# Second chunk's weights: the row term of the log sums as a bias of ScalarE, head by head

## The chip, the cores and the metric

The kernel runs on one core of a Trainium2 chip. The metric is the device time of one execution in microseconds; the times are medians over several runs, lower is better. The engines are called TensorE (PE in the profile, PEld its weight loads), VectorE (DVE), ScalarE (ACT), GpSimd (POOL) and SyncE (SP), which issues the DMAs.

## What is computed

An mLSTM over 4 batches, 8 heads, 768 steps and head size 40, and behind it a feed-forward layer with ELU (320 to 2048 to 320, over 3072 tokens). Cut to what matters:

```
for t in range(S):
    m_new  = max(f_gate[t] + m, i_gate[t])
    f_stab = exp(f_gate[t] + m - m_new);  i_stab = exp(i_gate[t] - m_new);  m = m_new
    C = f_stab * C + i_stab * outer(v[t], k[t])
    n = f_stab * n + i_stab * k[t]
    y[t] = sigmoid(o_gate[t]) * (C @ q[t]) / max(|n . q[t]|, 1)
h = x @ w_in                      # x: y with the heads side by side
out = elu(h) @ w_out
```

## The kernel before

The 768 steps are cut into six chunks of 128, and each chunk and batch is a tile, n = 4 * chunk + batch, so tiles 4 to 7 belong to the second chunk (c = 1). Inside a chunk the recurrence is written as attention: a tile multiplies keys by queries (`products`, L627: eight heads, in two PSUM buffers by parity of the head), multiplies that element by element by weights w[s, t] (L692), and multiplies the weighted products with the values (`outputs`, L712 for the state carried in, L720 inside the chunk, L730 for the state carried out). Then come the denominators (L764 to L769), the gate (L777, L781), a transpose by TensorE (`turn`, L795) and its split into a rounded and a rest part (xh, xl; L803 to L812, with L805 on TensorE in the first two tiles).

The weights of one head are w[s, t] = exp(a[t] + b[s]) for s <= t and 0 elsewhere, where a[t] is the running sum of the log decays and b[s] = i[s] - a[s]. For the first two chunks (LOGS = 2) they are made so. `gate_chunk` holds all 32 pairs of batch and head in the partitions and puts a into lc[:, 0] (L506) and b into lc[:, 1] (L510), 128 columns each. Because the matmuls that follow are in bf16, both are split into three bf16 parts, stacked in lcs (three casts, with two subtractions between them, L524; all of 256 columns). `spread`, once for each half of a tile (four heads), builds a + b + mask in a PSUM buffer of 512 columns: one matmul for the mask (L658), one for b, which picks the row of each head with the selection matrix sel (L662), and four of 128 columns for a (L668). One exponential on ScalarE (L683) then writes the half's weights to SBUF. Its last columns are copied to wl, and wl scales the values for the state (L696).

In the later chunks the weights come from a scan on VectorE (L675) and the source factors are transposed by TensorE (L542), copied to iT (steps in the partitions, batch and head in the columns) and multiplied into the values.

PSUM has three rings: ps_a with three buffers, h with two (the log sums of a half, the first layer's result h, and the differences of L379 and L380, which belong to the conversion of the weights) and acc with three (the opening matmuls L418, which only keep TensorE busy, and the second layer, L875).

The order of the instructions on each engine is no compiler's: every operation is handed to a planner with a cost for each engine that can do it (`op({"PE": 0.8}, ...)`), the keys that it reads and those that it writes. The planner runs a small simulation: at each moment it starts, of the operations that are ready, the one with the best rank (rank of the tile or conversion, then the longest rest of its chain), on the engine where it would start first. The order in which they start is the order of each engine's queue, and on the chip each engine works through its queue in order. Ranks of the first tiles and conversions stand in FIRST = "t0t1t2t4c5c0c4c3": tile 4 is begun before tile 3. Two of the conversions of w_in and w_out into a rounded and a rest part (L337 to L371 on ScalarE, VectorE and GpSimd, L379 and L380 with a difference on TensorE) are needed by each group of steps of the first layer (L848) and the second layer (L875).

Of the kernel before, what the change touches and what calls it, by code (L numbers as in the profile page):

```python
# [14 lines left out]
AF = mybir.ActivationFunctionType  # L15
# [5 lines left out]
P = 128  # L21
# [17 lines left out]
class Plan:  # L39
# [23 lines left out]
    def op(self, engines, fn, r=(), w=(), nbytes=0):  # L63
        port = "port" in engines
        engines = {e: x for e, x in engines.items() if e != "port"}
        o = Op(engines, fn, {k[:2] for k in (*r, *w)}, nbytes, port)
        o.rank = self.rank
        for k in r:
            if k in self.writer:
                o.before.add(self.writer[k])  # L70
            self.readers.setdefault(k, []).append(o)
        for k in w:
            if k in self.writer:
                o.before.add(self.writer[k])
            o.before.update(self.readers.pop(k, ()))
            self.writer[k] = o
        o.before.discard(o)
        for b in o.before:
            b.after.add(o)
        self.ops.append(o)  # L80
        return o
# [110 lines left out]
def tile_mlstm_then_elu_ffn(  # L192
# [9 lines left out]
    nc = tc.nc  # L202
    PSUM = bass.MemoryType.PSUM
    B, NC, R3, _, HH, L = qk.shape
# [4 lines left out]
    BH = B * H  # L209
# [7 lines left out]
    W2N = 2  # L217

    LOGS = 2
    LOG_MIN = -104.0  # L220
    MASKED = -(2.0**100)

# [19 lines left out]
    op = plan.op  # L242
    eng = {"PE": nc.tensor, "DVE": nc.vector, "ACT": nc.scalar, "POOL": nc.gpsimd, "SP": nc.sync}

    def copy(e, o, i):
        nc.scalar.copy(o, i) if e == "ACT" else eng[e].tensor_copy(o, i)
# [8 lines left out]
    def act(n):  # L255
        return {"ACT": 0.17 + 0.00088 * n}
# [213 lines left out]
    def gate_chunk(c):  # L470
        def f():
            return T("gates", c, BH, 2, L, part="fi")[:, 0]

        def i():
            return T("gates", c, BH, 2, L, part="fi")[:, 1]

        def m():
            return T("gates", c, BH, L + 1, part="m")

        KF, KI, KM, FI = ("gates", c, "f"), ("gates", c, "i"), ("gates", c, "m"), ("first", 0)  # L480

        op({"ACT": 0.2, "DVE": 0.13}, lambda e: copy(e, m()[:, 0:1], m0), (("m0", 0),), (KM,))
        op({"port": 1, "DVE": 0.48},
           lambda e: nc.vector.tensor_tensor_scan(
               m()[:, 1:], f(), i(), m0, op0=ALU.add, op1=ALU.max),
           (KF, KI, ("m0", 0)), (KM,))
        op({"ACT": 0.2, "DVE": 0.13}, lambda e: copy(e, m0, m()[:, L : L + 1]), (KM,), (("m0", 0),))

        def log_decay(e):
            nc.vector.tensor_add(f(), f(), m()[:, 0:L])  # L490
            nc.vector.tensor_sub(f(), f(), m()[:, 1:])
            if c < LOGS:
                nc.vector.tensor_scalar_max(f(), f(), LOG_MIN)

        op({"port": 1, "DVE": 0.6 if c >= LOGS else 0.84}, log_decay, (KM,), (KF,))
        op({"port": 1, "POOL": 0.4, "DVE": 0.27}, lambda e: eng[e].tensor_sub(i(), i(), m()[:, 1:]), (KM,), (KI,))
        if c < LOGS:

            def lc():
                return T("gates", c, BH, 2, L, part="lc")  # L500

            KLC = ("gates", c, "lc")

            def sums_of_logs(e):
                nc.vector.memset(lc()[:, 0, 0:1], 0.0)
                nc.vector.tensor_tensor_scan(  # L506
                    lc()[:, 0, 1:], f()[:, 1:], first[:, 1:], 0.0, op0=ALU.add, op1=ALU.min)

            op({"port": 1, "DVE": 0.53}, sums_of_logs, (KF, FI), (KLC,))
            op({"port": 1, "DVE": 0.27}, lambda e: nc.vector.tensor_sub(lc()[:, 1], i(), lc()[:, 0]), (KI,), (KLC,))  # L510
            if c > 0:
                op({"ACT": 0.35},
                   lambda e: nc.scalar.activation(i(), lc()[:, 0], AF.Exp, bias=f()[:, 0:1]), (KLC, KF), (KI,))
                op({"SP": 0.4}, lambda e: nc.sync.dma_start(b_d[c], i()), (KI,), (("b_d", c),),
                   nbytes=BH * L * 4)

            n = 2 * L
            for j in range(3):
                part = lcs[j * BH : (j + 1) * BH, c]
                op({"port": 1, "ACT": 0.2 + 0.00092 * n, "DVE": 0.29},  # L520
                   lambda e, part=part: copy(e, part, lc()), (KLC,), (("lcs", c, j),))
                if j < 2:
                    op({"port": 1, "DVE": 0.41},
                       lambda e, part=part: nc.vector.tensor_sub(lc(), lc(), part), (("lcs", c, j),), (KLC,))  # L524
            return
        op({"ACT": 0.3}, lambda e: nc.scalar.activation(f(), f(), AF.Exp), (), (KF,))
        op({"ACT": 0.3}, lambda e: nc.scalar.activation(i(), i(), AF.Exp), (), (KI,))

        def starts(e):

            nc.vector.tensor_copy(first[:, 0:1], f()[:, 0:1])
            nc.vector.memset(f()[:, 0:1], 0.0)

        op({"port": 1, "DVE": 0.2}, starts, (KF,), (FI, KF))
        op({"SP": 0.4}, lambda e: nc.sync.dma_start(f_d[c], f()), (KF,), (("f_d", c),),
           nbytes=BH * L * 4)

        def turned():
            return T("ps_a", ("iT", c), P, BH)

        KT = ("ps_a", ("iT", c))
        op({"PE": 0.24}, lambda e: nc.tensor.transpose(turned(), i(), ident[:BH, :BH]),  # L542
           (KI, ("ident", 0)), (KT,))
        op({"DVE": 0.19, "ACT": 0.25}, lambda e: copy(e, iT[:, c, :], turned()),
           (KT,), (("iT", c),))

        op({"port": 1, "DVE": 0.42},
           lambda e: nc.vector.tensor_tensor_scan(
               i(), f(), first, 0.0, op0=ALU.mult, op1=ALU.add),
           (KF, FI), (KI,))  # L550
        op({"SP": 0.4}, lambda e: nc.sync.dma_start(b_d[c], i()), (KI,), (("b_d", c),),
           nbytes=BH * L * 4)
# [32 lines left out]
    def attention(n):  # L585
# [18 lines left out]
        def w(half=None):  # L604
            a = T("w", n, P, H * L).rearrange("p (h t) -> p h t", t=L)
            return a if half is None else a[:, half * HH : (half + 1) * HH, :]
# [43 lines left out]
        for half in range(2):  # L650
            KW, KP = ("w", n, half), ("h", ("w", n, half))

            def logs(half=half):
                return T("h", ("w", n, half), P, HH, L)

            def spread(e, half=half, logs=logs):
                mine = [b * H + h for h in heads[half * HH : (half + 1) * HH]]
                nc.tensor.matmul(  # L658
                    logs(), ident_b, mask.unsqueeze(1).to_broadcast([P, HH, L]),
                    start=True, stop=False, skip_group_check=True,  # L660
                )
                nc.tensor.matmul(  # L662
                    logs(), lcs[:, c, 1],
                    sel[:, mine[0] : mine[-1] + 1 : 2].unsqueeze(2).to_broadcast([3 * BH, HH, L]),
                    start=False, stop=False, skip_group_check=True,
                )
                for j, r in enumerate(mine):
                    nc.tensor.matmul(  # L668
                        logs()[:, j, :], sel[:, r : r + 1].to_broadcast([3 * BH, P]), lcs[:, c, 0],
                        start=False, stop=(j == HH - 1), skip_group_check=True,  # L670
                    )

            def decays(e, half=half):
                a = w(half).rearrange("p h t -> p (h t)")
                nc.vector.tensor_tensor_scan(  # L675
                    a, a, ident4.rearrange("p h t -> p (h t)"), 0.0, op0=ALU.mult, op1=ALU.add
                )

            if c < LOGS:
                op({"PE": 0.8}, spread,  # L680
                   (("sel", 0), *(("lcs", c, j) for j in range(3)), ("mask", 0), ("ident_b", 0), ("w", n, "room")), (KP,))
                op(act(HH * L),
                   lambda e, half=half, logs=logs: nc.scalar.activation(w(half), logs(), AF.Exp), (KP,), (KW,))  # L683
            else:
                op({"port": 1, "DVE": 1.23}, decays, (("ident4", 0),), (KW,))

            if c < NC - 1:
                op({"POOL": 0.3, "DVE": 0.17, "ACT": 0.2},
                   lambda e, half=half: copy(e, wl()[:, half::2], w(half)[:, :, L - 1]),
                   (KW,), (("wl", n, half),))  # L690
            op(two_ps(HH * L),
               lambda e, half=half: nc.vector.tensor_mul(w(half), ps(half, P, HH, L), w(half)),  # L692
               (("ps_a", (n, half)),), (KW,))
# [319 lines left out]
```

## Time and profile before

| | us |
|---|---|
| median of 3 runs | 472.73 |
| lowest and highest of them | 469.61, 473.63 |
| the profiled execution's own time | 471.69 |
| its span in the profile | 469.8 |

The profile shows one execution. Its span goes from the first to the last instruction; the execution's own time has some 1.9 us more around it. Start times are in microseconds from the start of the span. "Idle before" is the time that an engine stood still in front of an instruction, with the instruction that ended the wait behind the arrow; "issue" means that nothing in the profile shows what it waited for. An arrow between two names (out<-in) says what is written from what.

### The profile page before, as it was taken

To read this page: it belongs to the slowest core of one execution; us is meant where nothing else is said; L and a number is where in the kernel's file an instruction comes from. 1 tells how busy PE (TensorE), PEld (TensorE's weight loads), DVE (VectorE), ACT (ScalarE), POOL (GpSimd) and SP (SyncE) were. 2 spreads that over 40 slices of the span, in tenths; PEclk is the share of its full clock that TensorE was granted. 3 is DMA by queue.
4 is the path that set the end of the run, shared out by engine and by line. 5 is a ranking of instruction groups with operands and counts; after the bars stand their busy time and mean duration, and the time that the engine had idled before them with its cause. 6 is when DMAs were issued, how large, how long until landed. Compare 5 with 4: busy or idle time off the path is not lost.

```text
span 469.8 us, 13709 instructions
## 1 busy us (share of the span) xinstructions
PE 454.2 (97%) x5700; PEld 426.3 (91%) x5700; DVE 340.0 (72%) x705; ACT 284.0 (60%) x701; POOL 94.7 (20%) x122
## 2 busy tenths in 40 slices
PE   6978999999999999999999999999999999999996
PEld 3757798999999999998899999999999999999995
DVE  6887888987878898688888885487448754464443
ACT  7776886688776547464654455545546455545563
POOL 2323353422311052234102220030010200000000
PEclk9888999999999999999999999999999999999999
DMA  8878644522407364248243532044113401000100
GB/s 241 312 209 269 190 153 143 179 100 95 140 2 220 97 189 128 74 155 228 64 142 108 161 119 83 1 129 127 42 31 102 144 1 43 0 3 1 43 0 31
DMA packets 39391, 52.85 MB, mean 112 GB/s; under 512 B 2880, under 2 KB 31264, under 8 KB 39328
## 3 DMA queue, kind: packets, MB, share of 16 engines
q1 hardware_dynamic: 39328, 51.97, 36.3%
q8 instruction: 45, 0.74, 0.7%
q14 instruction: 18, 0.15, 0.1%
HBM read 46.56 MB, written 5.39 MB: 111 GB/s over the span
## 4 chain that ended last, share of the span: by engine, by line
PE 88%; DVE 4%; ACT 3%; DMA 2%; issue 1%; SPq 0%; POOL 0%; POOLq 0%; ACTq 0%
PE h L848 37%; PE acc L875 35%; PE ps_a L627 5%; PE ps_a L720 3%; PE ps_a L712 3%; PE ps_a L795 2%; DMA wide<-in_w_in 2%; PE ps_a L730 1%; DVE gl L866 1%; ACT e L856 1%; ACT e L859 0%; DVE w L371 0%; PE h L379 0%; DVE w L675 0%; ACT narrow L337 0%
## 5 line engine op out<-in xcount | busy, mean ns | idle before, releaser
L848 PE MATMUL h<-xh,w 128*128 128x384 f32 (+1 forms) x720 | 178.8, 323 | 0.8 <-DVE e L861 0.8
L875 PE MATMUL acc<-w,gh 128*128 128x320 f32 x768 | 172.9, 311 | 1.4 <-ACT gh L864 0.9
L875 PEld LDWEIGHTS acc<-w,gh 128*128 128x128 f32 x768 | 128.2, 188 | 3.6 <-ACT gh L864 1.2
L848 PEld LDWEIGHTS h<-xh,w 128*128 128x128 f32 x720 | 125.4, 189 | 3.0 <-DVE e L861 1.3
L875 PE MATMUL acc<-w,gl 128*128 128x320 f32 x384 | 118.7, 309 | 1.2 <-DVE gl L866 1.2
L861 DVE SCALAR_TENSOR_TENSOR e<-e,h 128x384 f32<-128x384 f32 (+1 forms) x144 | 72.7, 506 | 62.4 <-ACT e L859 60.2
L856 ACT ACTIVATE e<-h 128x384 f32<-128x384 f32 (+1 forms) x144 | 65.4, 454 | 83.2 <-PE h L848 75.8
L848 PE MATMUL h<-xl,w 128*128 128x384 f32 (+1 forms) x432 | 112.0, 318 | 0.0
L866 DVE TENSOR_TENSOR gl<-e,gh 128x384 fp32r<-128x384 f32 (+1 forms) x130 | 70.8, 550 | 34.2 <-ACT gh L864 33.1
L864 ACT CAST gh<-e 128x384 fp32r<-128x384 f32 (+1 forms) x144 | 67.8, 474 | 33.3 <-DVE e L861 32.9
L848 PEld LDWEIGHTS h<-xl,w 128*128 128x128 f32 x432 | 77.0, 190 | 0.0
L875 PEld LDWEIGHTS acc<-w,gl 128*128 128x128 f32 x384 | 72.0, 188 | 1.7 <-DVE gl L866 1.7
L859 ACT ACTIVATE e<-e 128x384 f32<-128x384 f32 (+1 forms) x144 | 70.5, 490 | 3.5
L675 DVE TENSOR_TENSOR_SCAN w<-w,ident 128x512 f32<-128x512 f32 x32 | 40.5, 1275 | 0.4 <-DMA w<-f_d 0.3
L361 POOL TENSOR_TENSOR narrow<-narrow,wide 128x512 int32<-128x512 int32 (+1 forms) x18 | 27.4, 1520 | 60.5 <-DVE narrow L356 37.5
L747 POOL TENSOR_TENSOR C<-C,dec 40x164 f32<-40x164 f32 x26 | 14.5, 556 | 99.7 <-PE ps_a L712 96.9
L692 DVE TENSOR_TENSOR w<-ps_a,w 128x512 f32<-128x512 f32 x48 | 31.8, 682 | 2.8 <-PE ps_a L627 2.5
L627 PE MATMUL ps_a<-qk 40*128 40x128 f32 x384 | 29.0, 290 | 0.0
L627 PEld LDWEIGHTS ps_a<-qk 40*128 40x128 f32 x384 | 24.2, 192 | 4.5 <-issue 2.5
L866 POOL TENSOR_TENSOR gl<-e,gh 128x256 fp32r<-128x256 f32 (+1 forms) x14 | 12.4, 886 | 64.9 <-ACT gh L864 61.3
L720 PE MATMUL ps_a<-vko,w 128*32 128x41 f32 x1536 | 20.7, 207 | 0.3 <-DVE vko L637 0.3
L720 PEld LDWEIGHTS ps_a<-vko,w 128*32 128x32 f32 x1536 | 18.7, 114 | 1.7 <-issue 0.9
(113 smaller groups left out, 414.0 us busy)
## 6 DMA issues: line engine op xcount, KB each, us to landing
vko<-in_vko SPq DMA_DIRECT2D x24, 484.0 KB
qk<-in_qk SPq DMA_DIRECT2D x24, 448.0 KB
w<-f_d SPq DMA_DIRECT2D x32, 256.0 KB
wide<-in_w_out SPq DMA_DIRECT2D x8, 640.0 KB
wide<-in_w_in SPq DMA_DIRECT2D x8, 512.0 KB
out<-os SPq DMA_DIRECT2D x24, 160.0 KB
bb<-b_d SPq DMA_DIRECT2D x40, 80.0 KB
sum<-os SPq DMA_DIRECT2D x8, 160.0 KB
```

Source lines behind the costliest of these rows:

```text
L361: lambda e: nc.gpsimd.tensor_add(narrow(), narrow(), words()[0]),
L627: nc.tensor.matmul(ps(two, P, HH, L)[:, j, :], kt[rows, j, :], qt[rows, j, :], start=True, stop=True,)
L675: nc.vector.tensor_tensor_scan(a, a, ident4.rearrange("p h t -> p (h t)"), 0.0, op0=ALU.mult, op1=ALU.add)
L692: lambda e, half=half: nc.vector.tensor_mul(w(half), ps(half, P, HH, L), w(half)),
L720: nc.tensor.matmul(y[r, h, :], w()[:, i, r], va()[:, h, :], start=not opened, stop=(i == H - 1), skip_group_check=True,)
L848: nc.tensor.matmul(h(), a[g][:, fs], m, start=(i == 0), stop=(i == len(prods) - 1))
L856: op(act(N), lambda e, h=h, ff=ff: nc.scalar.activation(ff("e"), h(), AF.Relu, scale=-1.0), (KHP,), (KE,))
L859: lambda e, ff=ff: nc.scalar.activation(ff("e"), ff("e"), AF.Exp, scale=-1.0), (), (KE,))
L861: lambda e, h=h, ff=ff: nc.vector.scalar_tensor_tensor(out=ff("e"), in0=ff("e"), scalar=-1.0, in1=h(), op0=ALU.add, op1=ALU.max),
L864: op(act(N), lambda e, ff=ff: nc.scalar.copy(ff("gh", F32R), ff("e")), (KE,), (KG,))
L866: lambda e, ff=ff: eng[e].tensor_sub(ff("gl", F32R), ff("e"), ff("gh", F32R).bitcast(F32)),
L875: nc.tensor.matmul(acc(a), x[:, sl], bw[g][:, j, :], start=(f == f0 and i == 0), stop=(f == f1 - 1 and i == 2),)
```

## The change

For chunks from APART = 1 on that are weighted by log sums, which is the second chunk alone:

- only a, 128 columns of lc, is split into bf16 parts; the three casts and two subtractions run on half the columns, with their costs in the plan left as they were;
- b, in f32 as L510 leaves it, is transposed by TensorE into a buffer of the ring acc (cost in the plan 0.01) and copied by ScalarE to iT (0.01), as soon as L510 is done;
- `spread` leaves out the matmul of L662, its cost in the plan is unchanged;
- the exponential of a half is four instructions, one for each head, of 128 columns, with the head's column of iT as bias; the cost in the plan is that of the one instruction.

```
     LOGS = 2
+    APART = 1
...
+            apart = c >= APART
...
+            KLS = ("ls", c)
+            op({"port": 1, "DVE": 0.27}, lambda e: nc.vector.tensor_sub(lc()[:, 1], i(), lc()[:, 0]),
+               (KI,), (KLC, KLS))
...
-            n = 2 * L
+            n = L if apart else 2 * L
             for j in range(3):
-                part = lcs[j * BH : (j + 1) * BH, c]
-                op({"port": 1, "ACT": 0.2 + 0.00092 * n, "DVE": 0.29},
-                   lambda e, part=part: copy(e, part, lc()), (KLC,), (("lcs", c, j),))
+                part = lcs[j * BH : (j + 1) * BH, c, 0:1] if apart else lcs[j * BH : (j + 1) * BH, c]
+                op({"port": 1, "ACT": 0.2 + 0.00184 * L, "DVE": 0.29},
+                   lambda e, part=part: copy(e, part, lc()[:, 0 : n // L]), (KLC,), (("lcs", c, j),))
                 if j < 2:
                     op({"port": 1, "DVE": 0.41},
-                       lambda e, part=part: nc.vector.tensor_sub(lc(), lc(), part), (("lcs", c, j),), (KLC,))
+                       lambda e, part=part: nc.vector.tensor_sub(
+                           lc()[:, 0 : n // L], lc()[:, 0 : n // L], part), (("lcs", c, j),), (KLC,))
+            if apart:
+
+                def sources():
+                    return T("acc", "sources", P, BH)
+
+                KT = ("sources", c)
+                op({"PE": 0.01}, lambda e: nc.tensor.transpose(sources(), lc()[:, 1], ident[:BH, :BH]),
+                   (KLS, ("ident", 0)), (KT,))
+                op({"ACT": 0.01}, lambda e: copy(e, iT[:, c, :], sources()), (KT,), (("iT", c),))
...
-                nc.tensor.matmul(
-                    logs(), lcs[:, c, 1],
...
+                if c < APART:
+                    nc.tensor.matmul(
+                        logs(), lcs[:, c, 1],
...
-               op(act(HH * L),
-                  lambda e, half=half, logs=logs: nc.scalar.activation(w(half), logs(), AF.Exp), (KP,), (KW,))
+                def weigh(e, half=half, logs=logs):
+                    if c < APART:
+                        nc.scalar.activation(w(half), logs(), AF.Exp)
+                        return
+                    for j, r in enumerate(heads[half * HH : (half + 1) * HH]):
+                        nc.scalar.activation(w(half)[:, j], logs()[:, j], AF.Exp, bias=ib[:, r])
+
+                op(act(HH * L), weigh, (KP,) + ((("iT", c),) if c >= APART else ()), (KW,))
```

## Rows read from the trace of the kernel before

**Rows 1.** The page's first part: busy time of each engine, share of the span, number of instructions.

```profile
PE 454.2 (97%) x5700; PEld 426.3 (91%) x5700; DVE 340.0 (72%) x705; ACT 284.0 (60%) x701; POOL 94.7 (20%) x122
```

**Rows 2.** Two stretches of the span (from:to, length), with each engine's busy time and number of instructions, then TensorE's granted clock, the DMA engines' share and GB/s.

```profile
0.00:71.30 71.30, 61.52 (x1006) 46.25 (x1006) 56.37 (x143) 53.96 (x136) 23.72 (x34) 0.93 0.76 230
71.30:200.00 128.70, 128.64 (x1469) 125.65 (x1470) 107.85 (x218) 86.05 (x209) 36.85 (x38) 1.00 0.39 123
```

**Rows 3.** Pieces of the chain of work that ended last, from 27 to 43 us: start, how long the piece holds the chain, engine, tile, line and number of instructions.

```profile
27.44 1.25 PE ps_a L720 x64
28.69 0.59 PE ps_a L730 x32
...
35.26 0.22 PE h L662
...
38.08 0.74 PE ps_a L720 x64
38.82 0.29 PE ps_a L730 x32
...
40.95 1.88 issue
```

**Rows 4.** Groups of instructions by line, engine, operation and shape: number, busy time in us, mean ns of one, idle time before them. The second row is from the view of the one line L662: ns of the shortest, median and longest, first and last start.

```profile
L683 ACT ACTIVATE w<-h 128x512 f32<-128x512 f32 x16 | 9.2, 585 | 0.3 <-PE h L668 0.2
L662 PE MATMUL h<-sel,lcs x16: 379/381/534, 7.0 to 58.2; 96*128 96x512 bf16 x16
L513 ACT ACTIVATE gatesfi<-gateslc,gatesfi 32x128 f32<-32x128 f32 x1 | 0.4, 385 | 0.0
L526 ACT ACTIVATE gatesfi<-gatesfi 32x128 f32<-32x128 f32 x4 | 1.2, 298 | 0.1
L246 ACT COPY iT<-ps_a 128x32 f32<-128x32 f32 x3 | 0.5, 175 | 0.0
L542 PE MATMUL ps_a<-ident,gatesfi 32*128 32x32 f32 x4 | 1.0, 244 | 0.0
L524 DVE TENSOR_TENSOR gateslc<-gateslc,lcs 32x256 f32<-32x256 f32 x4 | 1.6, 412 | 0.1
L510 DVE TENSOR_TENSOR gateslc<-gatesfi,gateslc 32x128 f32<-32x128 f32 x2 | 0.6, 280 | 0.1
L246 DVE CAST lcs<-gateslc 32x256 bf16<-32x256 f32 x5 | 1.4, 272 | 0.1
```

**Rows 5.** Instructions in order of time, from 30 to 39 us: start, length (of the whole run where there are several), engine, line, operation, number, and idle time before it.

```profile
30.51 0.60 ACT L683 ACTIVATE w<-h 128x512 f32<-128x512 f32 x1
31.51 0.60 ACT L683 ACTIVATE w<-h 128x512 f32<-128x512 f32 x1
32.59 0.48 ACT L246 CAST xh<-ps_a 128x384 fp32r<-128x384 f32 x1 [0.26 <-PE ps_a L795]
34.88 0.38 PE L658 MATMUL h<-mask,ident_b 128*128 128x512 bf16 x1 [0.56 <-DVE w L246]
35.56 1.06 ACT L683 ACTIVATE w<-h 128x512 f32<-128x512 f32 x2
38.11 0.59 ACT L246 CAST w<-h 128x512 fp32r<-128x512 f32 x1 [1.26 <-PE h L380]
```

**Rows 6.** The same view from 22 to 30 us. The last row is the first spread of the second chunk.

```profile
22.39 1.57 PE L627 MATMUL ps_a<-qk 40*128 40x128 f32 x16
23.37 0.28 DVE L510 TENSOR_TENSOR gateslc<-gatesfi,gateslc 32x128 f32<-32x128 f32 x1
25.00 0.52 PE L795 MATMUL ps_a<-ident,xf 128*128 128x128 f32 x3 [1.04 <-DVE xf L781]
26.00 1.29 DVE L692 TENSOR_TENSOR w<-ps_a,w 128x512 f32<-128x512 f32 x2
26.24 0.46 ACT L246 CAST xh<-ps_a 128x384 fp32r<-128x384 f32 x1
26.75 0.69 PE L805 MATMUL ps_a<-xh,minus 128*128 128x384 f32 x1 [1.24 <-ACT xh L246]
29.17 0.61 PE L658 MATMUL h<-mask,ident_b 128*128 128x512 bf16 x1
```

**Rows 7.** The same view of ScalarE and TensorE alone, from 54 to 72 us.

```profile
54.85 0.62 ACT L367 CAST w<-narrow 128x512 fp32r<-128x512 f32 x1 [0.47 <-POOL narrow L361]
56.09 0.58 ACT L683 ACTIVATE w<-h 128x512 f32<-128x512 f32 x1
56.81 1.10 PE L379 MATMUL h<-narrow,ident 128*128 128x512 f32 x2
58.17 0.59 ACT L246 CAST w<-h 128x512 fp32r<-128x512 f32 x1 [0.79 <-PE h L380]
63.98 0.39 ACT L856 ACTIVATE e<-h 128x256 f32<-128x256 f32 x1 [0.88 <-PE h L848]
71.36 0.56 PE L875 MATMUL acc<-w,gh 128*128 128x320 f32 x2 [0.45 <-DVE w L371]
```

**Rows 8.** Three stretches, columns as in rows 2.

```profile
24.00:26.00 2.00, 0.52 (x3) 0.34 (x3) 1.87 (x8) 1.87 (x7) 0.00 (x0) 1.00 0.20 47
26.00:28.00 2.00, 1.25 (x39) 0.92 (x43) 1.96 (x4) 1.63 (x5) 0.00 (x0) 0.62 0.75 211
28.00:30.00 2.00, 2.00 (x78) 1.40 (x68) 1.18 (x3) 0.85 (x3) 1.28 (x1) 0.53 1.00 294
```

More of the change, by code (lines that the diff above doesn't have):

```diff
@@ L509, in gate_chunk @@
             op({"port": 1, "DVE": 0.53}, sums_of_logs, (KF, FI), (KLC,))
-            op({"port": 1, "DVE": 0.27}, lambda e: nc.vector.tensor_sub(lc()[:, 1], i(), lc()[:, 0]), (KI,), (KLC,))
+            KLS = ("ls", c)
+            op({"port": 1, "DVE": 0.27}, lambda e: nc.vector.tensor_sub(lc()[:, 1], i(), lc()[:, 0]),
+               (KI,), (KLC, KLS))
             if c > 0:
@@ L661, in spread @@
                 )
-                nc.tensor.matmul(
-                    logs(), lcs[:, c, 1],
-                    sel[:, mine[0] : mine[-1] + 1 : 2].unsqueeze(2).to_broadcast([3 * BH, HH, L]),
-                    start=False, stop=False, skip_group_check=True,
-                )
+                if c < APART:
+                    nc.tensor.matmul(
+                        logs(), lcs[:, c, 1],
+                        sel[:, mine[0] : mine[-1] + 1 : 2].unsqueeze(2).to_broadcast([3 * BH, HH, L]),
+                        start=False, stop=False, skip_group_check=True,
+                    )
                 for j, r in enumerate(mine):
```

## Prediction

> **What bounds the kernel now.** I read the page's busy times first: TensorE is busy for 97% of the span, ScalarE for 60% [rows 1]. An average over stages hides what matters here, so next I cut the span by stage. From 71.3 us on TensorE has no gap to speak of (128.64 busy of 128.70), and its clock is granted in full; before 71.3 us it is busy for 61.52 of 71.30 and has a granted clock of 0.93 [rows 2]. So the end comes at a fixed distance behind the moment at which TensorE gets into its stride, and only what shifts that moment moves the end. All work of the second chunk's weights lies before it: the eight spreads (tiles 4 to 7, two halves each) lie between 29.2 and 58.4 us [rows 4, 6]. In that stage the chain of waits changes between VectorE, ScalarE and TensorE, and so an edit pays only where it lies on this chain.
>
> **Prices.** What goes: eight matmuls of 512 columns. One occupies TensorE for 0.22 us before the next matmul starts [rows 3] (its own 381 ns overlap the neighbours [rows 4]): 8 x 0.22 = 1.76 us. What comes on TensorE: one transpose of 32x128, as the later chunks' transposes at 0.244 us [rows 4]. Net -1.5 us.
>
> VectorE: the two subtractions shrink from 256 to 128 columns, 0.412 to the 0.280 that a subtraction of 32x128 takes, 2 x -0.13. Of the three casts two are on VectorE at 0.272; halved they save between nothing and half of that, 0.14; I take -0.1 each; in all -0.45 us [rows 4]. ScalarE gets one copy of iT, 0.175 [rows 4], and its one cast of lcs gets about 0.1 shorter.
>
> ScalarE's exponentials are the large term. One half is now one instruction of 585 ns. It becomes four of 128 columns with a bias for each partition. The trace has no such form. The nearest rows are an exponential of 32x128 without a bias, 298 ns, and one of the same size with a bias from a column, 385 ns [rows 4]. Two exponentials in a row end 1.06 us after the first starts [rows 5], so neighbours overlap by 2 x 0.585 - 1.06 = 0.11. With the row that has a bias: 4 x 0.385 - 3 x 0.11 = 1.21, so +0.62 a half and +5.0 over eight. Lower end, the bias hidden behind the instruction before: 4 x 0.298 - 3 x 0.11 = 0.86, +0.28 a half and +2.2. Upper end, no overlap at all: 4 x 0.385 = 1.54, +0.96 a half and +7.7. Below nothing it can't go, as the same elements are read with three more starts. I take +0.62, the row that shares the form. By the Trainium skill (ScalarE: Activation LUTs, "What ACT_TABLE_LOAD costs"), each column operand adds some 93 ns and back-to-back instructions overlap by the same; an estimate from that page is 4 x 387 - 3 x 93 = 1.27 against 612 for the wide one, +0.66 a half and +5.3 in all. The rule speaks against the edit, and the trace shows 87 ns for the bias and 585 for the wide one.
>
> So by busy time the edit loses: 5 us of ScalarE for 1.5 of TensorE. What counts is where they fall.
>
> **From 22 to 30 us.** The transpose waits for the subtraction of L510, which ends at 23.65; TensorE reaches the products of the third tile (L627) at 22.39 [rows 6]. By the costs in the code the planner puts the transpose ahead of these products, because in its plan they start after that subtraction. Then TensorE, which works in order, stands still from 22.45 to 23.65, and the 16 products behind the transpose start at 23.9 and end at 25.5 in place of 23.96. Who waits for that? The transposes of L795 (25.00) move to 25.5, but their reader, the ScalarE cast of xh, starts only at 26.24, behind two conversion steps on its own engine. The multiplication L692 needs the products, and starts at 26.00 because VectorE is busy with the log sums until then; these get 0.45 shorter, so it can start at 25.55, just behind the products. So the stall is covered by the idle time of 1.04 before L795 and of 1.24 before L805 [rows 6], which the trace has anyway; without this cover it would cost 1.3. L692 ends 0.45 earlier, L805 stays where it is, and the outputs (L720, on the chain at 27.44) start 0.4 earlier. Bounds: 0 (the iT copy delays xh) to -0.45. I take -0.4. If the transpose stands behind the products, the result is the same. Its PSUM buffer comes from a ring that only the opening matmuls have used by then and the second layer uses later, so nobody waits for it.
>
> **From 30 to 43 us.** Tile 4's first exponential (30.51) is on the chain [rows 5]: -0.4 + 0.62 = +0.2 for the copy behind it and for the unbroken VectorE work up to the spread at 34.88. The second half (31.51) adds some 0.1 through the copy of its last column, since ScalarE has only 0.26 idle ahead of xh (32.59). The spread then starts 0.3 late, and with its row matmul gone it ends 0.1 late. Tile 5's two halves (35.56) add 1.24 to ScalarE, and the 1.26 that it waits at 38.11 for TensorE cover them [rows 5]. The stop of 1.88 us inside L712, with no releaser, I leave as it is [rows 3]: it starts in the middle of a block whose operands are there. So +0.1 at 43 us.
>
> **From 53 to 71 us.** Tile 6's first half costs 0.62 against 0.47 of idle time at 54.85: 0.15 is left [rows 7]. Its second half (56.09) is the place that counts: TensorE's L379 (56.81) takes the PSUM buffer that this exponential reads, of two in that ring, so it starts 0.7 late, and whatever the shorter spreads just before it saved is waited away there. Tile 7's first half is covered by the 0.79 that ScalarE waits at 58.17 for that same L379, now later too. Its second spread gives back 0.22, so +0.5 goes into the first layer; its second exponential (61.09) is covered by 0.88 of idle time at 63.98 [rows 7]. At 71.36 the second layer [rows 7] starts behind a conversion that hangs on the same ScalarE and VectorE work and is late by as much. From there TensorE hands it on to the end.
>
> Sum: -0.4 + 0.5 + 0.5 = +0.6 us. The profiled execution took 471.69 us (span 469.8 and 1.9 around it), so 472.3; the median of the runs shown lies 1.04 above it, which gives **473.3**. With the low price of the exponentials the sum is -0.3 (472.4 in medians), with the high one near +2 (474.7).
>
> **Rivals.**
> *The clock is kept: faster.* After TensorE was busy for only 0.52 of 2 us, its granted clock was 0.62 and then 0.53, near the lower of its two levels (1.2 of 2.4 GHz), from 26 to 30 us [rows 8]. The outputs took 1.25 and 0.59 there and 0.74 and 0.29 at 38 us in full clock [rows 3]. If the products that move into the gap keep the clock up, the chain gets 0.8 shorter: with the low price -0.3 - 0.8 = -1.1, 471.6. Against it: the gap isn't gone but lies earlier, and a fall at another place would cost as much. The Trainium skill (TensorE: Matmul & The Clock Gate, "Part 1: The HAM clock gate") says that the throttled state is the default and activity lifts it; by that less matmul work could lose clock, and here the fall behind the gap agrees.
> *ScalarE becomes the bound: slower.* It is one place, ScalarE's queue from 30 to 62 us. Where its idle time (0.26, 1.26, 0.47, 0.79 and 0.88 [rows 5, 7]) doesn't lie behind the halves that it has to cover, all +5.0 is on the path, less 0.4 and two row matmuls: +4.2, 476.9. It decides from about 0.8 a half on. For it speaks that exponentials hold buffers that TensorE wants; against it, that it still waits for other engines at these five places.
> *The order isn't what it was.* The new operations cost 0.01 in the plan, but a shift can swap neighbours. One swap is worth about one of the waits of this stage, 1.0 to 1.9 [rows 3, 6], either way: 471.4 to 475.2.
>
> **How the numbers follow.** Forecast 0.55, clock kept 0.2, ScalarE the bound 0.1, another order 0.12; 0.03 for the rest. The runs shown spread from 469.61 to 473.63, which is as wide as the cases, so the range goes beyond them a little: 470.2 to 477.0. A change below 1% (4.7 us) can't be told from none in a measurement of this kernel; beyond it on the slow side lie ScalarE's upper price and part of its rival (0.08), on the fast side a lucky order with a kept clock (0.04).
>
> **What would show it.** Exponentials of 128 columns near 0.38 us, 32 of them, and a half taking 1.2; TensorE idle before a transpose that ends near 23.9; L720 near 27.0; the spread of 34.88 near 35.2; L379 of 56.81 near 57.5 behind ScalarE; no gap of TensorE after 72. It is wrong if the second layer's unbroken run starts over 3 us away from 71.4, if a half takes under 0.8, or if TensorE's order before 70 us differs.

## The result and the profile after

| kernel | median, us | lowest to highest | runs |
|---|---|---|---|
| before | 472.74 | 468.49 to 474.58 | 22 |
| after | 476.04 | 472.83 to 478.87 | 22 |

The ratio is 1.0079, 95% interval 1.0054 to 1.0105. The change costs 3.3 us by the medians, 3.7 by the ratio. That is inside the predicted range and below 1%, but the sum said +0.6. The prediction held that a change below 1% can't be told from none in this kernel; with 22 runs on each side this one can.

The profiled execution of after took 472.83 us (span 470.7, granted clock 0.992). It is the shortest of its 22, so its span must not be set against that of before; what can be read from it are prices, order and gaps.

The page of after: first the busy times, to be read against [rows 1].

```profile
PE 452.3 (96%) x5693; PEld 424.6 (90%) x5693; DVE 339.2 (72%) x705; ACT 288.4 (61%) x726; POOL 94.8 (20%) x122
...
q8 instruction: 44, 0.72, 0.7%
```

TensorE has 7 matmuls and 7 weight loads fewer, ScalarE 25 instructions and 4.4 us more, as the edit says. The last row looks like nothing here (transfers, MB, share of 16 DMA engines' span); it is one of two queues of the kind "instruction", and the experiments will tie it to TensorE's program. Before has the row below. The 45th transfer of after starts behind the end of its span, at 471.83.

```profile
q8 instruction: 45, 0.74, 0.7%
```

Groups of after by line and shape, against [rows 4] (number, busy us, mean ns of one, idle time before):

```profile
L703 ACT ACTIVATE w<-h,iT 128x128 f32<-128x128 f32 x32 | 9.0, 370 | 0.0
L700 ACT ACTIVATE w<-h 128x512 f32<-128x512 f32 x8 | 4.6, 583 | 0.2
L528 DVE TENSOR_TENSOR gateslc<-gateslc,lcs 32x128 f32<-32x128 f32 x2 | 0.6, 276 | 0.0
L247 DVE CAST lcs<-gateslc 32x128 bf16<-32x128 f32 x2 | 0.4, 188 | 0.0
L536 PE MATMUL acc<-ident,gateslc 32*128 32x32 f32 x1 | 0.2, 243 | 0.0
```

The 32 new exponentials keep ScalarE busy for 9.0 us, where eight wide ones at 0.585 took 4.7.

Timeline of after from 22 to 39 us, rows against [rows 5] and [rows 6] (L641 is the old L627, L672 the old L658, L714 the old L692, L734 the old L712, L742 the old L720, L752 the old L730, L817 and L827 the old L795 and L805; L380 and L381 the old L379 and L380):

```profile
22.39 1.57 PE L641 MATMUL ps_a<-qk 40*128 40x128 f32 x16
...
24.98 0.52 PE L817 MATMUL ps_a<-ident,xf 128*128 128x128 f32 x3 [1.01 <-DVE xf L803]
...
25.42 0.24 PE L536 MATMUL acc<-ident,gateslc 32*128 32x32 f32 x1
25.63 1.29 DVE L714 TENSOR_TENSOR w<-ps_a,w 128x512 f32<-128x512 f32 x2
...
26.23 0.46 ACT L247 CAST xh<-ps_a 128x384 fp32r<-128x384 f32 x1
...
26.74 0.69 PE L827 MATMUL ps_a<-xh,minus 128*128 128x384 f32 x1 [1.07 <-ACT xh L247]
...
27.35 1.32 PE L742 MATMUL ps_a<-vko,w 128*32 128x41 f32 x64
```

The transpose (L536) follows the products and L817; nothing waits for it. L714 is 0.37 earlier than L692 was, and still the outputs start where they did, at 27.35 for 27.37; before has this row:

```profile
27.37 1.32 PE L720 MATMUL ps_a<-vko,w 128*32 128x41 f32 x64
```

```profile
30.49 1.14 ACT L703 ACTIVATE w<-h,iT 128x128 f32<-128x128 f32 x4
...
32.01 1.17 ACT L703 ACTIVATE w<-h,iT 128x128 f32<-128x128 f32 x4
```
```profile
35.65 0.38 PE L672 MATMUL h<-mask,ident_b 128*128 128x512 bf16 x1 [1.05 <-DVE w L247]
```
```profile
36.33 2.14 ACT L703 ACTIVATE w<-h,iT 128x128 f32<-128x128 f32 x8
...
38.91 0.59 ACT L247 CAST w<-h 128x512 fp32r<-128x512 f32 x1 [0.21 <-PE h L381]
```

A half takes 1.14 in place of 0.60. The spread of 34.88 starts at 35.65, and the idle time of 1.26 before the cast has shrunk to 0.21. The same view of ScalarE and then of TensorE from 55 us on, against [rows 7]:

```profile
55.67 1.12 ACT L703 ACTIVATE w<-h,iT 128x128 f32<-128x128 f32 x4
```
```profile
56.89 1.10 PE L380 MATMUL h<-narrow,ident 128*128 128x512 f32 x2 [1.10 <-issue]
```

TensorE stands still for 1.10 us until tile 6's exponentials release the buffer at 56.79. The view puts the wait down to "issue"; the end of the run above it, 55.67 + 1.12, is what the matmul follows.

Two stretches of after, the second to be set beside its row of before below:

```profile
71.30:200.00 128.70, 128.62 (x1468) 125.53 (x1469) 107.65 (x218) 85.85 (x209) 36.84 (x38) 1.00 0.40 123
160.00:215.00 55.00, 54.47 (x876) 51.72 (x875) 44.46 (x94) 29.41 (x91) 18.34 (x24) 1.00 0.49 147
```
```profile
160.00:215.00 55.00, 55.00 (x883) 52.45 (x882) 44.87 (x95) 30.10 (x92) 19.28 (x25) 1.00 0.50 151
```

Before has no gap of TensorE from 160 to 215 us; after has 0.53 us. Nearly all of it is one stop, in the middle of a block of equal matmuls, and the view shows nothing that TensorE waited for (timeline of TensorE, after and then before):

```profile
207.13 0.44 PE L752 MATMUL ps_a<-vko 128*8 128x41 f32 x25
208.09 0.27 PE L752 MATMUL ps_a<-vko 128*8 128x41 f32 x6 [0.51 <-issue]
```
```profile
206.94 0.49 PE L730 MATMUL ps_a<-vko 128*8 128x41 f32 x31
```

Matching the two traces instruction by instruction, after lies within 0.01 us of before all the way from 71 to 173 us, drops back by 0.2 at 174 and by 0.7 at 207, and keeps the difference to the end. That is new: a loss behind 72 us, where the change edits nothing and the prediction wanted no gap of TensorE.

That the second layer starts at 71.37 against 71.36, although 30 to 58 us lost time, has another cause. From 44 to 46 us the granted clock was 1.00 in this execution of after and 0.50 in that of before:

```profile
44.00:46.00 2.00, 2.00 (x54) 1.93 (x41) 1.28 (x5) 1.47 (x5) 0.82 (x1) 1.00 0.85 284
```
```profile
44.00:46.00 2.00, 2.00 (x30) 1.90 (x20) 1.28 (x5) 1.04 (x3) 0.05 (x1) 0.50 0.66 225
```

In 2 us of unbroken work it did 54 matmuls for 30. All runs taken together don't share this: the median of the granted clocks is 0.984 to 0.985 for after and 0.986 to 0.988 for before.

### The profile page after: what moved, and what is told of

It is laid out like the page before. It is cut to its first block, busy times and chain, and to the rows that moved or that the text cites. A ratio compares the mean times of both kernels' runs of the same rounds, so it can differ in the third digit from the quotient of the medians.

```text
span 470.7 us, 13721 instructions
## 1 busy us (share of the span) xinstructions
PE 452.3 (96%) x5693; PEld 424.6 (90%) x5693; DVE 339.2 (72%) x705; ACT 288.4 (61%) x726; POOL 94.8 (20%) x122
## 4 chain that ended last, share of the span: by engine, by line
PE 89%; DVE 4%; ACT 3%; issue 2%; DMA 1%; SPq 0%; ACTq 0%
PE h L870 37%; PE acc L897 36%; PE ps_a L641 5%; PE ps_a L742 3%; PE ps_a L734 3%; PE ps_a L817 2%; DMA wide<-in_w_in 1%; PE ps_a L752 1%; DVE w L372 0%; PE h L380 0%; ACT w L703 0%; DVE e L883 0%; ACT e L878 0%; DVE w L690 0%; DVE gl L888 0%
## 5 line engine op out<-in xcount | busy, mean ns | idle before, releaser
L714 DVE TENSOR_TENSOR w<-ps_a,w 128x512 f32<-128x512 f32 x48 | 31.8, 684 | 2.8 <-PE ps_a L641 2.5
L641 PE MATMUL ps_a<-qk 40*128 40x128 f32 x384 | 29.6, 291 | 0.3 <-issue 0.3
L641 PEld LDWEIGHTS ps_a<-qk 40*128 40x128 f32 x384 | 24.6, 192 | 5.0 <-issue 3.1
L742 PE MATMUL ps_a<-vko,w 128*32 128x41 f32 x1536 | 20.7, 207 | 0.3 <-DVE vko L651 0.3
L742 PEld LDWEIGHTS ps_a<-vko,w 128*32 128x32 f32 x1536 | 18.6, 114 | 1.7 <-issue 1.0
```

The lines of the kernel that those rows point to most:

```text
L641: nc.tensor.matmul(ps(two, P, HH, L)[:, j, :], kt[rows, j, :], qt[rows, j, :], start=True, stop=True,)
L742: nc.tensor.matmul(y[r, h, :], w()[:, i, r], va()[:, h, :], start=not opened, stop=(i == H - 1), skip_group_check=True,)
```

## The experiments

Three theories were in play. The exponentials alone (S): the sum of the prediction is right in kind, its sizes are off. The clock (K): after has another granted clock in most runs. The loads of TensorE's program (I): TensorE gets its program in blocks. The row of the queue supports blocks of 16 KB (0.74 MB in 45 transfers), about 255 instructions each if the 11,474 recorded instructions of TensorE (11,400 matmuls and weight loads, 74 semaphore waits and the like) fill 45 of them. The change takes 14 instructions of TensorE out of the program, so each later block boundary falls 14 instructions further on in the work; where it falls among many tiny matmuls, which use up a block in 2 to 6 us, the next block may come late and TensorE stops.

Ratios are against runs of the kernel before on the same chip, 95% intervals in brackets.

**Both kernels once more.** No edit.

> The changed kernel as it is, for its spread and its granted clock execution by execution. The profile at hand (472.83 us) is the lowest of 22 executions, whose median is 476.04, and its granted clock of 0.992 the highest of them. Theory S (ScalarE): the four exponentials with a bias are late by about 0.55 us a half, and this delay, at TensorE's PSUM buffers, is the whole 3.3 us; then a typical profile (475 to 477) has its TensorE waits before 71 us longer by that much at a granted clock that does not matter. Theory K (clock): the delays are below 1 us, and a typical profile has one or two more stretches at the lower clock between 25 and 60 us than the fast one, each worth 1 to 2 us. Both expect a median of 476 within 1.

> The kernel before as it is, for its granted clock execution by execution, which the runs at hand do not give. Theory S: the granted clock is spread as in the changed kernel (median about 0.984), so that clock tells nothing of the difference. Theory K: the median of the granted clock is higher than the changed kernel's by 0.003 or more, which at half speed is 1.4 us or more of span less at the lower clock for each 0.003. Both expect 472.7 within 1.

After: 475.35 us, 1.0068 [1.0033, 1.0103]. Before: 472.41 us, 0.9992 [0.9958, 1.0026]. So the loss is real and repeats. The clock is out as its main cause: the medians are 0.985 and 0.986, and a straight line of time against granted clock through the executions of both kernels puts after some 2.9 us behind before at equal clock. The second trace of after has its stop at another place, at 174 us instead of 207:

```profile
172.80 0.77 PE L742 MATMUL ps_a<-vko,w 128*32 128x41 f32 x63
174.42 0.20 PE L742 MATMUL ps_a<-vko,w 128*32 128x41 f32 x1 [0.85 <-issue]
```

The waits of TensorE in that trace show a second one at 207 us (us, times, longest):

```profile
PE ps_a L742 <- issue: 0.8, 1, 0.8
PE ps_a L752 <- issue: 0.5, 1, 0.5
```

Before runs through at this place, in one block after the other:

```profile
173.31 0.79 PE L720 MATMUL ps_a<-vko,w 128*32 128x41 f32 x64
173.90 0.49 PE L730 MATMUL ps_a<-vko 128*32 128x41 f32 x32
```

**The exponentials alone, first try.** The kernel before with 32 exponentials for the eight wide ones and a bias of zeros from a new column (L683):

```
+    zero = const.tile([P, 1], F32, name="zero")
...
+        nc.vector.memset(zero, 0.0)
...
-   nc.scalar.activation(w(half), logs(), AF.Exp)
+   for j in range(HH):                       # for c >= 1; the first chunk keeps its one
+       nc.scalar.activation(w(half)[:, j], logs()[:, j], AF.Exp, bias=zero)
```

> The kernel before with one part of the change alone: the exponential of a half of the second chunk is four instructions of 128 columns with a bias from a column of zeros; the row matmul, the 256-column splits and the plan stay. TensorE's and VectorE's work is that of before, ScalarE's that of the changed kernel. Theory S: all of the loss and a little more, since the savings are missing: 476.0 to 478. Theory K in its strict form (the missing columns are what costs the clock): at most 1 us over before, 472.7 to 473.7.

478.08 us, 1.0108 [1.0072, 1.0144]: more than the whole change. The trace says why this answers nothing: its lag behind before grows from 1.0 us at 71 us to 5.4 at the end, where no exponential was touched, and but for one stop of 1.07 us near 176 us it does so evenly. The new column moves every constant tile behind it by 4 bytes per partition.

**The column alone.** Before with the two "+ zero" lines and nothing else.

> The kernel before with an unused column of four bytes per partition in front of the constant tiles that follow, and nothing else. If the even growth is due to where the tiles lie: 476.5 to 477.5 and a lag that grows evenly by about 4.4 us from 75 to 463 us. If not: 472.7.

476.16 us, 1.0087 [1.0059, 1.0116]. The tile that nobody reads costs 4 us, again almost evenly: its lag goes from -0.9 at 75 us to +2.83 at 463. Eight matmuls of the first layer and nine of the second in the chain, column alone and then before:

```profile
303.25 1.41 PE h L850 x8
304.66 1.32 PE acc L877 x9
```
```profile
302.15 1.39 PE h L848 x8
303.54 1.31 PE acc L875 x9
```

So the run before this one was confounded by its own new column. The change itself adds no tile to SBUF; its one new tile, `sources`, lies in PSUM.

**The exponentials alone, without a new tile.** The bias is a column of the second chunk's part of iT, which the kernel before leaves unused, set to zero.

```
+        nc.vector.memset(iT[:, 1, :], 0.0)
...
+       nc.scalar.activation(w(half)[:, j], logs()[:, j], AF.Exp, bias=iT[:, 1, j : j + 1])
```

> The kernel before with the exponential of a half of the second chunk as four instructions with a bias of zeros, as one run before, but the zeros stand in a part of iT that is unused, so that no tile moves. In that earlier run the lag grew evenly by 4.4 us from 75 to 463 us, where both programs are the same, and at 71 us it was 1.0. Theory S with that drift as an artefact of the four new bytes in front of the other tiles: no even growth, 473.5 to 475.0. If the even growth belongs to the exponentials, 478 as before. Theory I adds nothing here, as TensorE's program is that of before.

473.27 us, 1.0028 [0.9999, 1.0057], about +1.3 us, and no even growth. The exponentials have the price that they have in after (view of the one line: number, shortest, median and longest ns):

```profile
L688 ACT ACTIVATE w<-h,iT x32: 347/368/412, 30.9 to 63.0; 128x128 f32<-128x128 f32 x32
```

This is the price of the exponentials without the savings of the change. It leaves more than half of the 3.3 to 3.7 us, though the interval reaches from nothing to 2.7 us.

**The row matmul's slot filled.** After, with a second matmul of the mask where the row matmul was, so that TensorE's program has about its old length (2 longer); the weights get the mask twice.

```
+                else:
+                    nc.tensor.matmul(logs(), ident_b, ...)     # the mask, as in the matmul before it
```

> The changed kernel with the mask added a second time in the place of the row matmul, so that TensorE streams as many columns in a spread as before; ScalarE's and VectorE's work is the changed kernel's, and the result is the same, as a doubled mask still gives 0. Theory S: as the changed kernel or slower by up to 0.6 (a matmul of 0.22 us comes back at two places of the chain): 476 to 476.7. Theory K: the clock comes back, 473 to 474.

473.98 us, 1.0025 [0.9999, 1.0051]. Here all of the change's own work is done and 1.76 us of TensorE's more than in after, and yet it is some 1.4 to 2 us faster than after. By itself this fits theory K as well, which had forecast 473 to 474.

**The program padded.** After with 7 matmuls of one column in the opening, which bring the program back to its old length and leave the spreads short.

```
+        few = T("acc", "spare", P, 512)
+        for _ in range(7):
+            nc.tensor.matmul(few[:, 0:1], ones, ones[:, 0:1], start=True, stop=True, ...)
```

> The changed kernel with seven matmuls of one column in the opening, so that TensorE's program behind the second chunk's spreads lies again where it lay before (the change takes seven weight loads and seven matmuls out of it). Theory I (instruction loads): in the traces TensorE stops inside blocks of tiny matmuls near 174 and 207 us in the changed kernel (0.2 to 1.0 and 0.7) and not in the kernel before, because the loads of 16 KB of its program fall at another place of the code; then both stops go, 0.9 to 1.7 us, and the median is 474.3 to 475.1. Theory S (ScalarE's exponentials are the whole loss): 475.4 to 476.0, unchanged, and the steps near 174 and 207 stay. Theory K (columns missing in the spreads cost clock): unchanged, too, since the columns stay away, while the variant that had the mask twice was at 474.0.

474.36 us, 1.0040 [1.0008, 1.0071]. It lies between; its interval overlaps that of after, so by itself it decides nothing. Its trace shows that a load can be late at the old place too, in a single execution (the stop is near 177 us, at the place where before runs through at 174):

```profile
PE ps_a L745 <- issue: 1.2, 1, 1.2
```

**The row matmul away, nothing else.** Before, in which the row matmul is issued for the first chunk only; this kernel leaves the source factor of the second chunk's weights out.

```
+                if c < 1:
                     nc.tensor.matmul(logs(), lcs[:, c, 1], ...)   # as in before
```

> The kernel before without the matmul that spreads the row term of the second chunk (its weights lack the factor of the source step); nothing else. Theory S: TensorE is 0.22 us ahead at two places of the chain, 471.8 to 472.5. Theory I: the program is 16 instructions shorter, as in the changed kernel, and the stops near 174 and 207 us come, +0.9 to 1.7: 473.2 to 474.2. Theory K: more stretches at the lower clock, 474 or more, without these stops.

475.11 us, 1.0065 [1.0040, 1.0090]. Taking eight matmuls (1.76 us of TensorE's time) away makes the kernel 3.1 us slower, with not one exponential changed. Its stop of 0.97 us stands at 174 us, in the same group of tiny matmuls as that of the second run of after:

```profile
173.74 0.79 PE L721 MATMUL ps_a<-vko,w 128*32 128x41 f32 x64
175.50 0.50 PE L731 MATMUL ps_a<-vko 128*32 128x41 f32 x32 [0.97 <-issue]
```

**The same with the program's length restored.** The kernel above with 8 matmuls of one column in the opening, written as in the padded kernel; the source factor is left out as there.

> The kernel before without the row matmul of the second chunk (its weights lack the factor of the source step), and with eight matmuls of one column in the opening, so that TensorE's program has its old length behind the second chunk. The same without these eight was at 1.0065 of before, although it only leaves work out; its trace stops TensorE for 0.5 and 1.2 us near 169 and 174 us and for 1.1 near 47 in the middle of blocks, always at an instruction whose number is 193 above a multiple of 256. Theory I (place of the program's loads): ratio 0.996 to 1.001. Theory K (missing columns cost clock): 1.005 to 1.007, as the columns are still missing.

472.78 us, 1.0014 [0.9982, 1.0046]. Beside 1.0065 [1.0040, 1.0090] without the eight the loss is gone, and so is the stop in that block:

```profile
175.00 0.79 PE L724 MATMUL ps_a<-vko,w 128*32 128x41 f32 x64
175.59 0.49 PE L734 MATMUL ps_a<-vko 128*32 128x41 f32 x32
```

This pair is the cleanest test: same work in the spreads, same everything on the other engines. What differs is the place of the later program, the eight tiny matmuls in the opening and the PSUM buffer that they write. It speaks against theory K too: the columns are missing in both, and the median granted clock is 0.985 to 0.986 in both. The two ran on different chips, each beside before.

**The program moved the other way.** Before and after with the opening's filler work cut (EARLY_WORK 10 to 8) and matmuls of one column put in its place, so that the later program stands 38 instructions further back than in before. From the boundaries of the first traces I had worked out that none would fall into a block that is used up in a few us at 41, 174 or 207 us.

```
-    EARLY_WORK = 10
+    EARLY_WORK = 8
...
+        few = T("acc", "spare", P, 512)
+        for _ in range(21):                   # 28 in the kernel made from after
+            nc.tensor.matmul(few[:, 0:1], ones, ones[:, 0:1], start=True, stop=True, ...)
```

> The kernel before with its program moved by 38 instructions against the blocks of 256: two of the ten opening matmuls go and 21 of one column come. In the kernel before the block that ends at instruction 1217 stops TensorE for 2.1 us near 41 us. By the times of the trace of before a boundary 38 instructions earlier leaves the load some 2 us more before it is needed. Theory I: the stop near 41 us goes or shrinks to under 1, the sum of the stops falls from 2.1 to 1 or less, ratio 0.994 to 0.999. If the place of the loads doesn't matter, 1.000.

> The changed kernel with its program moved to the same place as in the run above (28 matmuls of one column in the opening, two of the ten wide ones go). Theory I: it loses only what the exponentials cost, as the exponentials alone did (1.0028): 0.998 to 1.003 of before. Theory S: 1.007, as the changed kernel.

476.98 us, 1.0101 [1.0057, 1.0145], and 476.52 us, 1.0104 [1.0069, 1.0140]. The first was expected to be faster than before, the second to be level with it; both missed. The boundaries moved, but the stops went to other blocks, one of them to 170 us, where before has none:

```profile
170.20 0.24 PE L733 MATMUL ps_a<-vko 128*32 128x41 f32 x3 [1.19 <-issue]
```

That place matters, these runs support; which place is good, I could not compute. They also change the opening itself, so not all of their 4.2 to 4.6 us need be stops.

**All stops side by side.** I numbered all recorded instructions of TensorE (matmuls, weight loads, semaphore waits) from 0 in the order of their starts, and list each gap, from start to start, of at least 0.2 us in front of number 193 + 256 k, without the last of these numbers, where the kernels end. The stops without a releaser (the profile shows nothing that was waited for) inside blocks of tiny matmuls all stand at such a number; a few others, at 1473 and 1985, stand among the larger matmuls of the two layers:

```
kernel          records  number: stop in us                          sum   ratio
before           11474   1217: 2.11                                  2.1   1
before again     11474   1217: 2.19                                  2.2   0.9992
filled           11476   1217: 2.18                                  2.2   1.0025
exps_only        11474   1217: 0.37  1473: 1.15  5313: 0.53          2.0   1.0028
padded           11474   1217: 0.70  4289: 1.38                      2.1   1.0040
no_row_padded    11474   1217: 0.42  1473: 1.67  5313: 0.26          2.4   1.0014
after            11460   1217: 1.73  1473: .54  4289: .22  5313: .71 3.2   1.0079
after again      11460   1217: 2.08  1473: .34  4289: 1.05 5313: .73 4.2   1.0068
no_row           11458   1217: .80  1473: 1.11  4033: .53
                         4289: 1.17  8129: .24                       3.8   1.0065
before_moved     11512   1217: 1.46  1473: 2.32  4033: 1.39          5.2   1.0101
after_moved      11512   1217: 1.81  1473: 2.41  1985: 0.35          4.6   1.0104
shifted          11474   1217: 1.57                                  1.6   1.0087
exps_alone       11474   1217: 2.07  1473: 0.38  4289: 1.07          3.5   1.0108
```

Each line is one execution, and the two last have the cost of the moved constants besides. The others fall into three groups by the place of their program, and a larger sum goes with a larger ratio from group to group, though not inside one: the old place 2.0 to 2.4 us, 14 to 16 instructions shorter 3.2 to 4.2, 38 longer 4.6 to 5.2. The place doesn't decide alone: exps_alone has the old place and 3.5 us.

Behind 75 us, where the programs do the same work, the lag behind before grows by 0.9 us in after and 1.8 in its second trace, by 1.8 in no_row, 0.3 in no_row_padded and not at all in the second trace of before. That is what the stops there add up to (0.9, 1.8, 1.9, 0.3 and none), so these stops reach the end of the kernel one for one.

The traces also time each transfer of the queue q8, and there are as many transfers as such numbers (one fewer in the second trace of after). Taking them in order, each as the block of program behind the next boundary (us; arrival is the start of the last instruction before the boundary):

```
kernel          number  transfer            TensorE arrives, goes on
before          1217     40.22 to  41.41     40.72   42.83
before          4289    170.91 to 171.98    173.81  173.82
before          5313    204.71 to 205.65    207.09  207.09
after           5313    205.74 to 206.70    207.38  208.08
after again     4289    171.49 to 172.82    173.38  174.42
no_row          4289    172.81 to 173.99    174.33  175.50
no_row_padded   4289    172.44 to 173.54    175.49  175.50
```

In the 13 traces TensorE never goes on less than 1.2 us behind the end of the transfer, however early it arrives. Of the 34 stops listed, 33 end 1.2 to 1.6 us behind it; the 0.24 of no_row at 8129 does not. The transfers belonging to these 33 stops started 0.4 to 4.5 us behind the boundary before; what decides this delay the runs don't show, and without it the good place can't be computed.

## Why the prediction came out as it did

The time fell into the range, and "within 1%" held. That is owed to the width of the range: the sum's 473.3 was 2.7 us short. The mechanism of the sum held in two of its three stages; a term was missing that is as large as the rest.

*Price of the exponentials: right.* A half was to cost +0.62 and cost 1.14 - 0.60 = +0.54; over eight that is +4.3 of ScalarE's time against the 5.0 taken. One takes 370 ns, near the row with a bias (385) that I chose as the nearest. The Trainium skill (ScalarE: Activation LUTs, "What ACT_TABLE_LOAD costs") led to an estimate of 1.27 a half; the trace has 1.14.

*22 to 30 us: -0.4 was to come and did not.* VectorE did get 0.37 earlier. But TensorE takes the outputs in order behind L827, and L827 waits for the copy of xh, which stayed at 26.23. The text had said that L805 "stays where it is" and let the outputs behind it move all the same. The transpose stands behind L817 and not ahead of the products; that the result would be the same held.

*30 to 43 us: +0.5 predicted (from -0.4 to +0.1), +0.8 measured ahead of the stop.* The spread of 34.88 came 0.77 later instead of 0.3, because both halves of tile 4 lie on the chain that leads to it. The cover of 1.26 us at 38.11 had shrunk to 0.21, since L380 itself came late, at 37.54 for 36.72. (Behind it, up to 50 us, this execution of after gains 1.2 us back, from +0.8 to -0.4: its stop at 41.75 is shorter and its clock stays up at 44 us. The second trace of after, its clock up as well, gains 1.1 there.)

*53 to 71 us: +0.5 predicted, +0.5 measured.* TensorE's L380 waits 1.10 us for tile 6's exponentials, and the lag of after behind before goes from -0.41, ahead of the spread at 51 us, to +0.09 at L380 and +0.01 at 71 us.

Put together: 0 + 0.8 + 0.5 = +1.3 for the change's own terms against +0.6. The exponentials alone, without the change's savings, measured +1.3 as well (1.0028, from nothing to +2.7). This part of the loss is understood in kind, its size to a microsecond or so.

*The step that failed.* "The stop of 1.88 us inside L712, with no releaser, I leave as it is", and with it "only what shifts that moment moves the end". The stop was on the chain in full view [rows 3], and it belongs to a kind that the change touches: it stands at a boundary of TensorE's program, and the change moves this boundary and all later ones. In after it is 1.50 us long (a piece of the chain), and the boundaries at 47, 174 and 207 us now stop TensorE as well:

```profile
41.75 1.50 issue
```

The stops add up to 3.2 and 4.2 us in the two traces of after against 2.1 and 2.2 in those of before, +1.0 to +2.1. With the +1.3 of the change's own terms that makes +2.3 to +3.4, beside the 3.3 to 3.7 measured. This is no full account: both traces of after are of executions among its shortest, with the clock granted at 0.992 and 0.993, and none of the longer ones was traced.

How far this is shown: the pair without the row matmul (1.0065 and 1.0014) shows that the program's place is worth about 2.4 us (the ratios differ by 0.0051, give or take 0.0041); the stops behind 75 us in both traces of after and in no_row, and nearly none in no_row_padded, show where. That a late transfer of the program is the cause rests on the numbers 193 + 256 k, on the 16 KB of a transfer and on the times of the transfers, behind whose ends the stops end. No run made the transfer itself faster. The Trainium skill (Runtime: NRT & Kernel Launch, "Instruction fetch mechanics") states the same block, 16 KiB or 256 instructions, and says that the cost of crossing a boundary is "mostly hidden". The first agrees with the trace. Of the second: 40 or more of some 45 boundaries in each trace show no stop, but the one to five others lie bare, with up to 2.41 us each.

*The rivals.* The clock kept: not what decided the time. The medians of the granted clocks lie 0.001 to 0.004 apart, after's being the lower, and at equal clock some 2.9 us of the loss are left; the gap before L817 is as long as it was (1.01 for 1.04). ScalarE as the bound: no, its +4.3 us cost about 1.3. Another order: each engine issues its instructions in the order of before, apart from those added and removed. The slow side was thus near the rivals' times (475.2 to 476.9) and for none of their reasons.

## What to carry to other kernels

A stop with no releaser in the middle of a block of equal instructions is not part of the scenery: number the instructions up to it, see whether the stop ends behind a transfer of the instruction queue, and if the numbers are equal modulo a constant in several places, every instruction that a change adds to or takes from that engine ahead of it is part of the change's price. Before an effect under 1% is put down to the edit, run the edit once more with the length of the program and the place of the tiles held as they were. An engine's idle time is cover for new work only if the instruction that ends it doesn't itself start later through that work.

## What the runs showed of the hardware

Fewer matmuls can take longer: eight matmuls less made the kernel 1.0065 as long, and eight matmuls of one column in the opening took this back (1.0014).

TensorE's program comes in transfers of 16,384 bytes, one for each 256 recorded instructions. In 13 traces TensorE went on at such a boundary 1.2 us or more behind the end of the transfer, and where it arrived earlier it stopped, for up to 2.41 us; blocks that it used up in 2 to 6 us were the ones at risk.

Four bytes per partition, written once and read by nobody, cost 1.0087 [1.0059, 1.0116]. Runs of matmuls of both layers got about 1% longer (1.39 to 1.41 us for eight, 1.31 to 1.32 for nine). That it is the place of the tiles behind the column follows from the kernel, which differs in nothing else but one memset; why the place matters to TensorE stays open. The kernel with a bias from a tile that was there already has no such growth.
